# Query projections of an attention and expert kernel: from three split products over 128 rows to raw fp32 products over 64 rows

## The chip, the cores and the metric

The kernel runs on one core of one Trainium2 chip. A core has five engines that run side by side, each with its own instruction stream in a fixed order: TensorE (matrix products, PE in the profile, its loading of the stationary operand PEld), VectorE (DVE), ScalarE (ACT), GpSimd (POOL) and SyncE (SP, which issues loads). The metric is device time in microseconds (us) of one execution. Three runs of the kernel before took 596.02, 597.88 and 600.78 us; the median is 597.88.

## What is computed

```python
def phi(x):                                    # q, k, v: 4 batches x 8 heads x 576 x 64
    proj = np.einsum('bhsd,df->bhsf', x, w_phi)            # w_phi: 64 x 128
    proj = proj - np.max(np.abs(proj), axis=-1, keepdims=True)
    return np.concatenate([np.exp(proj), np.exp(-proj)], axis=-1)
q_p, k_p = phi(q), phi(k)
kv = np.einsum('bhsf,bhsd->bhfd', k_p, v)
z = np.sum(k_p, axis=2)
x = np.einsum('bhsf,bhfd->bhsd', q_p, kv) / (np.einsum('bhsf,bhf->bhs', q_p, z)[..., None] + 1e-06)
...                                            # heads joined: x is 4 x 576 x 512
gate = sigmoid(causal depthwise convolution of x, 5 taps)
x = (gate * (x @ w_val)) @ w_out
...                                            # one of 8 experts for each token, by running argmax
out = p[e] * (np.maximum(x @ w1[e], 0.0) @ w2[e])
```

The change is in `proj` of the queries alone. All inputs and results are fp32.

## The kernel before

The 4 x 576 tokens are 18 tiles of 128. `qT` and `kT` lie with the channels (8 heads x 64) on the rows, so a tile `raw` is 128 rows x 4 chunks x 128 tokens, and each chunk holds two heads one above the other. `wraw` holds `w_phi` twice on its diagonal (128 x 256, zeros elsewhere), so that one product over 128 rows projects both heads of a chunk. A half tile (`hh`) is four heads: two chunks, a result `pj` of 128 tokens x 512 in one bank of PSUM.

**Keys.** For each half tile two products of `raw` with `wraw` (line 129) in raw fp32, then on VectorE the largest absolute value (`m`, line 132) and its subtraction (`pp`, line 134), on ScalarE two exponentials (`ex`), and on TensorE `kv` (line 159), products of 64 columns, which add up over a batch.

**Queries.** The same projection, but each operand is split in two parts in a shorter format (fp32r): `split` casts a raw tile on ScalarE (`qkh`, line 49) and subtracts on GpSimd (`qkl`, line 52), and `wb_hi` and `wb_lo` are the parts of `wraw`. Three products then stand for one: hi x hi, hi x lo, lo x hi. A half tile takes six products of 128 rows, 128 stationary and 256 moving columns. After `m` and `pp` come four transposes (`tp`, line 186), the exponentials, the numerator and denominator (`num`, line 198, 64 columns) and the division. When both halves of a tile are done, `xp` (line 225) transposes its rows.

**Mixing.** Beside the queries run the convolution (VectorE, GpSimd, ScalarE), `vps` (line 400, x times `w_val` in three split products) and `yps` (line 535, gate times `w_out`). Small products `lpp`, `lps` and `wps` make the logits; `lpp` (line 432) writes one of four groups of 32 columns in each product. Then tokens are sorted by expert, gathered, and the expert stage (`hp`, line 857, and `op`, line 871) runs to the end.

**What sets the order.** `run` walks through the half tiles, first all keys, then all queries: the projection of half tile i + 3, the transposes of i + 1, the numerator of i, and some of the mixing. A scheduler then orders each engine's instructions by when it thinks that their operands are ready, so the order on an engine is not the order in the text. `pj` of the queries has two banks (`ps_p`, `bufs=2`), one for each half; `raw` has four buffers, and a tile's load is issued three tiles ahead (`loads_to`).

Of the kernel before, what the change touches and what calls it, by code (L numbers as in the profile page):

```python
# [8 lines left out]
F32 = mybir.dt.float32  # L9
F32R = mybir.dt.float32r  # L10
# [9 lines left out]
B, H, S, DH, DF = 4, 8, 576, 64, 128  # L20
T, D, E, FF, KC = 2304, 512, 8, 1024, 5
NT = T // 128
# [15 lines left out]
def body(ctx, tc, qT, kT, v1, wbd, w_val, conv_w, w_out, w_gl, w1, w2, out):  # L38
    nc = tc.nc
    V, A, G, PE, SP = nc.vector, nc.scalar, nc.gpsimd, nc.tensor, nc.sync  # L40
# [7 lines left out]
    def hi_of(eng, hi, src):  # L48
        (A.copy if eng is A else eng.tensor_copy)(hi, src)  # L49

    def lo_of(eng, lo, src, hi):
        eng.tensor_tensor(lo, src, hi.bitcast(F32), ALU.subtract)  # L52
# [21 lines left out]
    ap = attx.enter_context(tc.tile_pool(name="ap", bufs=1))  # L74
    ps_p = psx.enter_context(tc.tile_pool(name="ps_p", bufs=2, space=PSUM))
    ps_a = psx.enter_context(tc.tile_pool(name="ps_a", bufs=2, space=PSUM))
    ps_c = psx.enter_context(tc.tile_pool(name="ps_c", bufs=1, space=PSUM))
    ps_b = psx.enter_context(tc.tile_pool(name="ps_b", bufs=3, space=PSUM))

    wraw = ap.tile([128, 256], F32, name="wraw")  # L80
    wb_hi = ap.tile([128, 256], F32R, name="wb_hi")
    wb_lo = ap.tile([128, 256], F32R, name="wb_lo")

    raw_t, hl_t, v_t = {}, {}, {}

    def load(nm, t):
        if t >= NT or (nm, t) in raw_t:
# [14 lines left out]
        v_t[t] = mp.tile([128, H * VW], F32, tag=("gp", "gv")[t % 2], name="v", bufs=2)  # L102
        SP.dma_start(v_t[t], v1[t * 128:(t + 1) * 128, :])

    def split(nm, t):

        if t >= NT or (nm, t) in hl_t or nm == "k":
            return
        hi = ap.tile([128, 4, 128], F32R, tag="qkh", name="qkh", bufs=2)
        lo = ap.tile([128, 4, 128], F32R, tag="qkl", name="qkl", bufs=2)  # L110
        hi_of(A, hi, raw_t[nm, t])
        lo_of(G, lo, raw_t[nm, t], hi)
        hl_t[nm, t] = (hi, lo)

    def proj(nm, t, hh):
        raw = raw_t[nm, t]
        if nm == "k" and hh == 1:
            pj = ps_b.tile([128, 4, 128], F32, tag="b", name="pj")
        else:
            pj = ps_p.tile([128, 4, 128], F32, tag="pj", name="pj")  # L120
        for cc in range(2):
            c = 2 * hh + cc
            o = pj[:, 2 * cc:2 * cc + 2, :].rearrange("p h f -> p (h f)")
            prods = ((raw, wraw),)
            if (nm, t) in hl_t:
                hi, lo = hl_t[nm, t]
                prods = ((hi, wb_hi), (hi, wb_lo), (lo, wb_hi))
            for i, (st, mv) in enumerate(prods):
                PE.matmul(o, lhsT=st[:, c, :], rhs=mv, start=(cc == 0 and i == 0),  # L129
                          stop=(cc == 1 and i == len(prods) - 1), skip_group_check=True)  # L130
        m = ap.tile([128, 4], F32, tag="m", name="m", bufs=3)
        V.tensor_reduce(m, pj, axis=AX.X, op=ALU.max, apply_absolute_value=True)  # L132
        pp = ap.tile([128, 4, 128], F32, tag="pp", name="pp", bufs=3)
        V.tensor_tensor(pp, pj, m.unsqueeze(2).to_broadcast([128, 4, 128]), ALU.subtract)  # L134
        return pp
# [9 lines left out]
    def pk(t, hh):  # L145
        kp_t[t, hh] = both_exp(proj("k", t, hh))
# [32 lines left out]
    def pq(t, hh):  # L179
        pq_t[t, hh] = proj("q", t, hh)  # L180
# [63 lines left out]
    def bg(n, m=0):  # L244
        for i in range(n + m):
            if bgq and i < n:
                bgq.pop(0)()
            elif bg2 and len(done) == 4:
                bg2.pop(0)()
# [302 lines left out]
    st = {"step": 0, "credit": 0.0}  # L552
# [28 lines left out]
    order = []  # L581
# [4 lines left out]
    ahead = {i: (i + LF) // 2 for i in range(-LF, len(items))}  # L586

    def loads_to(i):
        for kind, t in order[:i + 1]:
            load(kind, t)  # L590
# [14 lines left out]
    def run(nbg, rate):  # L605
        n = len(items)
        txq = []
        for i in range(-LF, n + 3):
            st["step"] += 1
            if i == 1:  # L610
                setup_small()
            if 1 < i <= 5:
                setup_w("val", w_val, i - 2)
            if 0 <= i + LF < n:
                kind, t, hh = items[i + LF]
                if hh == 0:
                    loads_to(ahead[i] + 3)
                    for z in order[:ahead[i] + 2]:
                        split(*z)
                if kind == "k":  # L620
                    pk(t, hh)
                else:
                    pq(t, hh)
            if 0 <= i + 1 < n and items[i + 1][0] == "q":
                tq(*items[i + 1][1:])
            while txq and txq[0][0] <= i:
                t = txq.pop(0)[1]
                tx(t)
                if t % 2 == 1:
                    push_mix(t // 2)  # L630
            if 0 <= i < n:
                back(i)
                if items[i][0] == "q" and items[i][2] == 1:
                    txq.append((i + 2, items[i][1]))
            bg(*nbg(i))
            fill(rate(i))
# [3 lines left out]
    make_identity(nc, ident)  # L640
    load_v(0)
    loads_to(1)
    hi_of(V, wb_hi, wraw)
    lo_of(V, wb_lo, wraw, wb_hi)
    route_consts()
    run(lambda i: (0, 0) if i < 0 else ((i + 1) * 13 // 10 - i * 13 // 10, 0) if i < 36 else (5, 2), lambda i: 2.2 if i > 38 else 0)
    attx.close()
# [5 lines left out]
    for item in vq:  # L653
        what, z = item[3] or (None, 0)
# [84 lines left out]
    lo = t_([128, NT], "lo", BF16)  # L739
# [16 lines left out]
    for t in range(NT):  # L756
        pin(PE.matmul(tab.rearrange("p a c -> p (a c)"), lhsT=ohl[:, t, :], rhs=ohc[:, t].rearrange("p a c -> p (a c)"),
                  start=(t == 0), stop=(t == NT - 1)))
# [214 lines left out]
```

## Time and profile before

| what | value |
|---|---|
| profiled execution | 596.02 us, of which 594.2 us of span |
| key stage, 0 to 88.0 us | TensorE busy 81.35 us |
| query stage, 88.0 to 238.2 us (first to last query product) | TensorE busy 148.47 us |
| rest of the mixing, to 313.2 us | TensorE busy 74.41 of 75.00 us |
| gathers, to 331 us | TensorE busy 14.11 of 17.80 us |
| experts, to the end | TensorE busy 251.60 of 263.00 us |

A record of the timeline says when an instruction started and how long it took from its start to its end. TensorE's steps overlap, so the distance from one start to the next, and not the duration, is what a step costs the stream. A shape such as 128*64 128x65 is 128 rows x 64 stationary columns, and 128 rows x 65 moving columns. Equal records that follow each other are merged (x32); the start is that of the first.

### The profile page before, as it was taken

Reading aid. Unit: us, or ns where it says so; the run is one execution under the profiler, and the core shown is the slowest. Engines: PE = TensorE matmul, PEld = TensorE weight load, DVE = VectorE, ACT = ScalarE, POOL = GpSimd, SP = SyncE. Lnnn points to the kernel's source line nnn. Section 1 sums busy time; section 2 is a strip of 40 time slices with the busy share of each in tenths; the row PEclk is TensorE's granted clock in tenths of the full one; section 3 lists DMA queues with packets and bytes.
Section 4 is the critical chain, followed back from the end, with each engine's and each line's share of the span. In section 5 each row is a group of like instructions: output and inputs, shape, how many; then the busy total and the mean of one; then the engine's idle time right before and its main releaser. Section 6 shows DMA issues by size and latency. Waiting matters only on the chain. (4 is left out here: it accounts for less than half of the span.)

```text
span 594.2 us, 13524 instructions
## 1 busy us (share of the span) xinstructions
PE 569.9 (96%) x5477; PEld 495.5 (83%) x5478; DVE 365.2 (61%) x726; ACT 313.1 (53%) x573; POOL 238.0 (40%) x258
## 2 busy tenths in 40 slices
PE   7999999999999999999997999999999999999993
PEld 6777788898889889888784988889889899898982
DVE  5888689478687876569613766555666656452110
ACT  3767566466665575565323656445655646541210
POOL 2453055388778885583124022322340322311001
PEclk9999999899999999999998899999999999999997
DMA  8934431111101000221524887758668649620000
GB/s 281 311 99 122 130 107 49 32 33 38 36 4 35 3 38 21 72 77 48 198 90 132 302 268 217 239 190 269 210 211 272 202 138 291 203 95 36 17 19 36
DMA packets 46017, 76.82 MB, mean 129 GB/s; under 512 B 3839, under 2 KB 22399, under 8 KB 45952
## 3 DMA queue, kind: packets, MB, share of 16 engines
q1 hardware_dynamic: 39840, 60.55, 32.8%
q0 software_dynamic: 3520, 10.58, 4.7%
q10 hardware_dynamic: 2592, 4.79, 2.1%
q8 instruction: 45, 0.74, 0.5%
q14 instruction: 20, 0.16, 0.1%
HBM read 66.39 MB, written 10.56 MB: 130 GB/s over the span
## 5 line engine op out<-in xcount | busy, mean ns | idle before, releaser
L857 PE MATMUL hp<-xh,w1h 128*128 128x256 f32 (+1 forms) x320 | 94.6, 296 | 1.4 <-DVE hlo L860 0.8
L857 PE MATMUL hp<-xh,w1l 128*128 128x256 f32 (+1 forms) x320 | 93.8, 293 | 0.0
L857 PE MATMUL hp<-xl,w1h 128*128 128x256 f32 (+1 forms) x320 | 93.3, 294 | 0.0
L815 POOL DMA_INDIRECT xg<-y_d,gidx x22 | 36.7, 1669 | 98.5 <-DVE p L838 83.4
L877 POOL DMA_INDIRECT out<-osb,sidx x22 | 28.0, 1271 | 115.1 <-ACT osb L876 69.0
L871 PE MATMUL op<-w2h,hh 128*128 128x512 f32 x176 | 69.5, 400 | 1.0 <-ACT hh L859 0.9
L52 DVE TENSOR_TENSOR w2l<-wraw,w2h 128x1024 fp32r<-128x1024 f32 x40 | 48.8, 1223 | 34.5 <-ACT w2h L49 34.3
L860 DVE SCALAR_TENSOR_TENSOR hlo<-hp,hh 128x256 fp32r<-128x256 f32 (+1 forms) x80 | 34.2, 446 | 55.4 <-ACT hh L859 55.4
L871 PE MATMUL op<-w2l,hh 128*128 128x512 f32 x176 | 68.2, 393 | 0.0
L871 PE MATMUL op<-w2h,hlo 128*128 128x512 f32 x176 | 67.0, 394 | 0.0
L857 PEld LDWEIGHTS hp<-xh,w1h 128*128 128x128 f32 x320 | 61.2, 191 | 3.9 <-DVE hlo L860 1.2
L52 DVE TENSOR_TENSOR w1l<-wraw,w1h 128x1024 fp32r<-128x1024 f32 x40 | 48.7, 1251 | 24.1 <-ACT w1h L49 24.1
L857 PEld LDWEIGHTS hp<-xh,w1l 128*128 128x128 f32 x320 | 61.1, 191 | 1.4
L857 PEld LDWEIGHTS hp<-xl,w1h 128*128 128x128 f32 x320 | 60.7, 191 | 0.0
L132 DVE TENSOR_REDUCE m<-pj 128x4 f32<-128x512 f32 x72 | 49.3, 686 | 18.4 <-PE pj L129 17.5
L266 DVE SCALAR_TENSOR_TENSOR acc<-xT,tfs,acc 128x256 f32<-128x256 f32 (+1 forms) x112 | 53.8, 485 | 10.8 <-ACT acc L264 9.7
L859 ACT ACTIVATE hh<-hp 128x256 fp32r<-128x256 f32 (+1 forms) x80 | 31.4, 403 | 53.8 <-PE hp L857 53.6
L49 ACT CAST w2h<-wraw 128x1024 fp32r<-128x1024 f32 x40 | 41.8, 1050 | 31.7 <-DMA wraw<-w 22.3
L49 ACT CAST w1h<-wraw 128x1024 fp32r<-128x1024 f32 x40 | 40.3, 1049 | 24.6 <-DMA wraw<-w 24.5
L159 PEld LDWEIGHTS kv<-v,ex 128*64 128x64 f32 (+1 forms) x1280 | 40.7, 137 | 14.7 <-issue 6.8
L134 DVE TENSOR_TENSOR pp<-pj,m 128x512 f32<-128x512 f32 x72 | 49.4, 686 | 4.4 <-PE tp L186 1.8
L159 PE MATMUL kv<-v,ex 128*64 128x65 f32 (+1 forms) x1280 | 46.1, 224 | 3.0 <-DVE kvsb L171 1.4
(194 smaller groups left out, 1332.5 us busy)
## 6 DMA issues: line engine op xcount, KB each, us to landing
wraw<-w SPq DMA_DIRECT2D x80, 512.0 KB, 4.5
v<-v SPq DMA_DIRECT2D x18, 260.0 KB, 3.2
y_d<-ysb ACTq DMA_DIRECT2D x18, 260.0 KB, 2.1
raw<-qT SPq DMA_DIRECT2D x18, 256.0 KB, 2.9
raw<-kT SPq DMA_DIRECT2D x17, 256.0 KB, 4.2
wr<-w_val SPq DMA_DIRECT2D x4, 512.0 KB, 5.9
wr<-w_out SPq DMA_DIRECT2D x4, 512.0 KB, 6.9
xg<-y_d,gidx POOLq DMA_INDIRECT x22, 5.4
```

Source lines behind the costliest of these rows:

```text
L49: (A.copy if eng is A else eng.tensor_copy)(hi, src)
L52: eng.tensor_tensor(lo, src, hi.bitcast(F32), ALU.subtract)
L132: V.tensor_reduce(m, pj, axis=AX.X, op=ALU.max, apply_absolute_value=True)
L134: V.tensor_tensor(pp, pj, m.unsqueeze(2).to_broadcast([128, 4, 128]), ALU.subtract)
L159: PE.matmul(kv_ps[b][blk // 7][mh * 64:mh * 64 + 64, (blk % 7) * VW:(blk % 7 + 1) * VW], lhsT=kp_t[t, hh][off:off + n, sg, h, mh * 64:mh * ...
L266: W["tap"] = V.scalar_tensor_tensor(acc[c], xs, cw[:, kk, c:c + 1], acc[c], ALU.mult, ALU.add)
L815: G.indirect_dma_start(out=xg, out_offset=None, in_=y_d, in_offset=bass.IndirectOffsetOnAxis(ap=gc, axis=0))
L857: PE.matmul(hp[:, 0:n], lhsT=wt[:, k, f * 128:(f + 1) * 128], rhs=xt[:, k, 0:n], start=(i == 0), stop=(i == 11))
L859: A.activation(hh[:, f, 0:n], hp[:, 0:n], AF.Relu)
L860: low = V.scalar_tensor_tensor(hlo[:, f, 0:n], hp[:, 0:n], 0.0, hh[:, f, 0:n].bitcast(F32), ALU.max, ALU.subtract)
L871: PE.matmul(op, lhsT=ht[:, f, sl], rhs=wt[:, f, :], start=(i == 0), stop=(i == 23))
L877: G.indirect_dma_start(out=out, out_offset=bass.IndirectOffsetOnAxis(ap=scols[j], axis=0), in_=osb, in_offset=None, bounds_check=T - 1, oo ...
```

## The change

The splits of the queries are gone: `split`, `qkh`, `qkl`, `wb_hi` and `wb_lo`, one cast on ScalarE and one subtraction on GpSimd for each tile, and two operations on VectorE at the start. The queries are projected in raw fp32. The host lays `qT` out so that chunk c holds head c in rows 0 to 63 and head 4 + c in rows 64 to 127. Each product takes 64 rows of the array, 128 stationary columns (the tokens) and 128 moving columns (`w_phi`), and the two halves of a tile write two banks. All eight products of a tile are issued with its first half, in turn upper and lower. The keys are as they were.

```diff
@@ -78,10 +78,8 @@
     ps_b = psx.enter_context(tc.tile_pool(name="ps_b", bufs=3, space=PSUM))
 
     wraw = ap.tile([128, 256], F32, name="wraw")
-    wb_hi = ap.tile([128, 256], F32R, name="wb_hi")
-    wb_lo = ap.tile([128, 256], F32R, name="wb_lo")
-
-    raw_t, hl_t, v_t = {}, {}, {}
+
+    raw_t, v_t = {}, {}
 
     def load(nm, t):
         if t >= NT or (nm, t) in raw_t:
@@ -102,32 +100,29 @@
         v_t[t] = mp.tile([128, H * VW], F32, tag=("gp", "gv")[t % 2], name="v", bufs=2)
         SP.dma_start(v_t[t], v1[t * 128:(t + 1) * 128, :])
 
-    def split(nm, t):
-
-        if t >= NT or (nm, t) in hl_t or nm == "k":
-            return
-        hi = ap.tile([128, 4, 128], F32R, tag="qkh", name="qkh", bufs=2)
-        lo = ap.tile([128, 4, 128], F32R, tag="qkl", name="qkl", bufs=2)
-        hi_of(A, hi, raw_t[nm, t])
-        lo_of(G, lo, raw_t[nm, t], hi)
-        hl_t[nm, t] = (hi, lo)
+    pj_t = {}
+
+    def products(nm, t, hh):
+        raw = raw_t[nm, t]
+        if nm == "k":
+            pool, tag = ((ps_p, "pj"), (ps_b, "b"))[hh]
+            pj = pj_t[hh] = pool.tile([128, 4, 128], F32, tag=tag, name="pj")
+            for cc in range(2):
+                o = pj[:, 2 * cc:2 * cc + 2, :].rearrange("p h f -> p (h f)")
+                PE.matmul(o, lhsT=raw[:, 2 * hh + cc, :], rhs=wraw, start=(cc == 0), stop=(cc == 1), skip_group_check=True)
+        elif hh == 0:
+
+            for z in range(2):
+                pj_t[z] = ps_p.tile([128, 4, 128], F32, tag="pj", name="pj")
+            for c in range(4):
+                for z in range(2):
+                    rows = slice(z * 64, z * 64 + 64)
+                    PE.matmul(pj_t[z][:, c, :], lhsT=raw[rows, c, :], rhs=wraw[rows, z * DF:z * DF + DF],
+                              start=(c == 0), stop=(c == 3), skip_group_check=True)
 
     def proj(nm, t, hh):
-        raw = raw_t[nm, t]
-        if nm == "k" and hh == 1:
-            pj = ps_b.tile([128, 4, 128], F32, tag="b", name="pj")
-        else:
-            pj = ps_p.tile([128, 4, 128], F32, tag="pj", name="pj")
-        for cc in range(2):
-            c = 2 * hh + cc
-            o = pj[:, 2 * cc:2 * cc + 2, :].rearrange("p h f -> p (h f)")
-            prods = ((raw, wraw),)
-            if (nm, t) in hl_t:
-                hi, lo = hl_t[nm, t]
-                prods = ((hi, wb_hi), (hi, wb_lo), (lo, wb_hi))
-            for i, (st, mv) in enumerate(prods):
-                PE.matmul(o, lhsT=st[:, c, :], rhs=mv, start=(cc == 0 and i == 0),
-                          stop=(cc == 1 and i == len(prods) - 1), skip_group_check=True)
+        products(nm, t, hh)
+        pj = pj_t.pop(hh)
         m = ap.tile([128, 4], F32, tag="m", name="m", bufs=3)
         V.tensor_reduce(m, pj, axis=AX.X, op=ALU.max, apply_absolute_value=True)
         pp = ap.tile([128, 4, 128], F32, tag="pp", name="pp", bufs=3)
@@ -615,8 +610,6 @@
                 kind, t, hh = items[i + LF]
                 if hh == 0:
                     loads_to(ahead[i] + 3)
-                    for z in order[:ahead[i] + 2]:
-                        split(*z)
                 if kind == "k":
                     pk(t, hh)
                 else:
@@ -640,8 +633,6 @@
     make_identity(nc, ident)
     load_v(0)
     loads_to(1)
-    hi_of(V, wb_hi, wraw)
-    lo_of(V, wb_lo, wraw, wb_hi)
     route_consts()
     run(lambda i: (0, 0) if i < 0 else ((i + 1) * 13 // 10 - i * 13 // 10, 0) if i < 36 else (5, 2), lambda i: 2.2 if i > 38 else 0)
     attx.close()
@@ -946,7 +937,9 @@
     import concourse.bacc as bacc
     from concourse.bass_utils import run_bass_kernel_spmd
 
-    def chan(a):
+    def chan(a, paired=False):
+        if paired:
+            a = a[:, [h // 2 + h % 2 * (H // 2) for h in range(H)]]
         return np.ascontiguousarray(a.transpose(1, 3, 0, 2).reshape(H * DH, T))
 
     ones = np.ones((B, S, H, 1), dtype=v.dtype)
@@ -955,7 +948,7 @@
     wbd[:DH, :DF] = w_phi
     wbd[DH:, DF:] = w_phi
     arrays = {
-        "qT": chan(q), "kT": chan(k), "v1": v1, "wbd": wbd,
+        "qT": chan(q, True), "kT": chan(k), "v1": v1, "wbd": wbd,
         "w_val": np.ascontiguousarray(moe_w_val).view(np.int64),
         "conv_w": np.ascontiguousarray(moe_conv_w.reshape(KC, 4, 128).transpose(2, 0, 1).reshape(128, KC * 4)).view(np.int64),
         "w_out": np.ascontiguousarray(moe_w_out).view(np.int64),
```

The scheduler moves instructions. Two places on TensorE show how. The first is the first query tile, at the border of keys and queries. In the names, `kv` are the key sums, `pj` the projections with their buffer's number; before:

```order
L159 MATMUL kv1_1162<-v_984,ex_1223 64x65 x2
L129 MATMUL pj_1351<-wb_hi_94,qkh_1276 128x256
L129 MATMUL pj_1351<-wb_lo_95,qkh_1276 128x256
L129 MATMUL pj_1351<-wb_hi_94,qkl_1277 128x256
L129 MATMUL pj_1351<-wb_hi_94,qkh_1276 128x256
L129 MATMUL pj_1351<-wb_lo_95,qkh_1276 128x256
L129 MATMUL pj_1351<-wb_hi_94,qkl_1277 128x256
L159 MATMUL kv1_1162<-v_984,ex_1254 64x65 x12
```

and now, where `pj_1339` is the upper half's result (heads 0 to 3) and `pj_1340` the lower half's:

```order
L154 MATMUL kv1_1158<-v_980,ex_1219 64x65 x2
L120 MATMUL pj_1339<-wraw_93,raw_1111 128x128
L120 MATMUL pj_1340<-wraw_93,raw_1111 128x128
L120 MATMUL pj_1339<-wraw_93,raw_1111 128x128
L120 MATMUL pj_1340<-wraw_93,raw_1111 128x128
L120 MATMUL pj_1339<-wraw_93,raw_1111 128x128
L120 MATMUL pj_1340<-wraw_93,raw_1111 128x128
L120 MATMUL pj_1339<-wraw_93,raw_1111 128x128
L120 MATMUL pj_1340<-wraw_93,raw_1111 128x128
L154 MATMUL kv1_1158<-v_980,ex_1250 64x65 x12
```

The products of both halves now stand at the place of the first half's, in turn, as in the text.

The second place is the sixth query tile on TensorE; `num` is the numerator of an earlier half tile, `tp` and `xp` are transposes. Before:

```order
L129 MATMUL pj_1874<-wb_hi_94,qkh_1741 128x256
L129 MATMUL pj_1874<-wb_lo_95,qkh_1741 128x256
L129 MATMUL pj_1874<-wb_hi_94,qkl_1742 128x256
L198 MATMUL num_1718<-kvsb_526,ex_1662 64x65 x16
L186 MATMUL tp_1756<-ident_61,pp_1655 128x128 x4
L225 MATMUL xp_1764<-ident_61,x_1618 128x128 x2
L129 MATMUL pj_1973<-wb_hi_94,qkh_1741 128x256
L129 MATMUL pj_1973<-wb_lo_95,qkh_1741 128x256
L129 MATMUL pj_1973<-wb_hi_94,qkl_1742 128x256
```

and now (`pj_1822` is the upper half's, `pj_1823` the lower half's):

```order
L181 MATMUL tp_1715<-ident_61,pp_1622 128x128 x4
L220 MATMUL xp_1723<-ident_61,x_1586 128x128 x2
L120 MATMUL pj_1822<-wraw_93,raw_1505 128x128 x4
L193 MATMUL num_1747<-kvsb_522,ex_1674 64x65 x16
L181 MATMUL tp_1782<-ident_61,pp_1667 128x128 x4
L120 MATMUL pj_1823<-wraw_93,raw_1505 128x128 x4
L220 MATMUL xp_1848<-ident_61,x_1677 128x128 x2
```

Here the scheduler has parted the two halves: four products of the upper half, other work, then four of the lower. Over the 18 tiles, five have all eight products in turn as in the first place (one of them with `num` before the last two), one has four in turn and four in pairs of one half, three have four of one half directly before four of the other, one has three directly before four, and in eight other work stands between the halves' blocks. From the first to the last query product the array's shape (whole, 64 columns, 32 columns, 64 rows) changes 97 times in the order before and 119 times in this; if 64 rows and the whole array are counted as one shape, 89 times.

## Rows read from the trace of the kernel before

**Rows 1.** The page, part 1: busy us, share of the span, instructions.

```profile
PE 569.9 (96%) x5477; PEld 495.5 (83%) x5478; DVE 365.2 (61%) x726; ACT 313.1 (53%) x573; POOL 238.0 (40%) x258
```

**Rows 2.** Stretches: start:end, length, busy (count) by engine, TensorE clock, DMA share, GB/s.

```profile
0.00:88.00 88.00, 81.35 (x1337) 65.16 (x1337) 66.95 (x111) 57.44 (x103) 31.62 (x52) 1.00 0.57 175
88.00:238.20 150.20, 148.47 (x1913) 132.83 (x1911) 114.18 (x274) 91.27 (x199) 109.88 (x122) 0.99 0.10 30
238.20:313.20 75.00, 74.41 (x611) 60.39 (x610) 44.25 (x126) 34.15 (x70) 31.81 (x42) 1.00 0.29 100
...
108.80:112.20 3.40, 3.40 (x26) 3.25 (x26) 1.46 (x4) 0.97 (x3) 0.00 (x0) 0.50 0.19 53
112.20:116.00 3.80, 3.80 (x57) 3.41 (x57) 2.67 (x7) 2.86 (x6) 1.33 (x2) 1.00 0.00 0
```

**Rows 3.** Groups by line, 88 to 238.2 us: count, busy us, mean ns, idle before.

```profile
L129 PE MATMUL pj<-wb_hi,qkh 128*128 128x256 f32 x72 | 22.7, 315 | 1.7 <-DVE pp L134 1.7
L129 PE MATMUL pj<-wb_lo,qkh 128*128 128x256 f32 x72 | 20.6, 287 | 0.0
L129 PE MATMUL pj<-wb_hi,qkl 128*128 128x256 f32 x72 | 20.4, 284 | 0.0
```

**Rows 4.** Waits of TensorE, 88 to 238.2 us: total us, times, longest.

```profile
PE pj L129 <- DVE pp L134: 1.7, 4, 0.6
```

**Rows 5.** Timeline of TensorE, two places: start us, us.

```profile
87.99 0.39 PE L129 MATMUL pj<-wb_hi,qkh 128*128 128x256 f32 x1
...
88.89 1.15 PE L159 MATMUL kv<-v,ex 128*64 128x65 f32 x32
89.97 0.39 PE L129 MATMUL pj<-wb_hi,qkh 128*128 128x256 f32 x1
...
237.17 0.28 PE L129 MATMUL pj<-wb_hi,qkh 128*128 128x256 f32 x1
...
237.88 0.39 PE L535 MATMUL yps<-wout_h,gh 128*128 128x512 f32 x1
```

**Rows 6.** Timeline of TensorE around the steps of nine columns.

```profile
104.08 1.85 PE L372 MATMUL wps<-wgl,woT 128*128 128x9 f32 x16
105.78 0.36 PE L129 MATMUL pj<-wb_hi,qkh 128*128 128x256 f32 x1
```

**Rows 7.** Timeline of TensorE: raw products, runs over 64 rows, column quarters.

```profile
26.78 1.13 PE L129 MATMUL pj<-wraw,raw 128*128 128x256 f32 x4
27.84 1.15 PE L159 MATMUL kv<-v,ex 64*64 64x65 f32 x32
28.92 1.13 PE L129 MATMUL pj<-wraw,raw 128*128 128x256 f32 x4
...
34.59 2.35 PE L159 MATMUL kv<-v,ex 64*64 64x65 f32 x68 [0.76 <-DVE kvsb L171]
36.87 0.48 PE L129 MATMUL pj<-wraw,raw 128*128 128x256 f32 x1
...
75.92 3.17 PE L159 MATMUL kv<-v,ex 64*64 64x65 f32 x96
79.02 0.48 PE L129 MATMUL pj<-wraw,raw 128*128 128x256 f32 x1
...
149.14 0.64 PE L432 MATMUL lpp<-gv,wl 128*32 128x256 f32 x8
149.71 0.39 PE L129 MATMUL pj<-wb_hi,qkh 128*128 128x256 f32 x1
```

**Rows 8.** Groups by line, whole span: the keys' projection.

```profile
L129 PE MATMUL pj<-wraw,raw 128*128 128x256 f32 x144 | 42.2, 425 | 3.6 <-DMA raw<-kT 3.6
```

**Rows 9.** Groups by line, 88 to 238.2 us: the queries' splits.

```profile
L49 ACT CAST qkh<-raw 128x512 fp32r<-128x512 f32 x16 | 10.1, 632 | 2.6 <-POOL tmw L323 1.2 <-PE pj L129 1.0 <-issue 0.4
L52 POOL TENSOR_TENSOR qkl<-raw,qkh 128x512 fp32r<-128x512 f32 x16 | 21.0, 1310 | 4.9 <-ACT qkh L49 4.9
```

## The prediction

> **What bounds the kernel now.** First the busy shares: TensorE 96%, VectorE 61% [rows 1]. Then the stages. The query stage, from the first query product at 88.0 us to the last at 238.2 us, has 148.47 us of TensorE work in 150.20 us, the rest of the mixing after it 74.41 in 75.00 [rows 2]. A busy TensorE need not be one at its peak, so I next read its waits there: one line, four waits for VectorE's `pp`, 1.7 us in all [rows 4]. No wait there names ScalarE, GpSimd or a load. So TensorE bounds the query stage by its own instruction stream, and what is put into that stream or taken out arrives at the end of the stage one for one. The next stage is filled by the same engine, and the gathers and the expert stage come after it, so the end moves as well. This case is a count of TensorE steps.
>
> The steps must be read as start to start, since their durations overlap: six query products between steps that also use the whole array take 237.88 - 237.17 = 0.71 us, 0.118 each, though each is recorded as about 0.28 [rows 3, 5].
>
> **The change part by part.**
>
> *Taken out of TensorE.* 3 x 72 = 216 records of query products [rows 3] at 0.118 = **-25.5 us**.
>
> *Put in.* 18 tiles x 8 = 144 raw products, each over 64 rows and 128 columns. A raw fp32 product runs as two records: the keys' 72 left 144 [rows 8]. So 288 records. The price of one: four raw records of 256 columns between column-split steps take 27.84 - 26.78 = 1.06 us [rows 7]; six query products in such a place take 88.89 - 87.99 = 0.90, against 0.71 elsewhere [rows 5], so 0.19 of it is entry and exit, and a record is (1.06 - 0.19) / 4 = 0.22 for 256 columns, 0.11 for 128. Loading 128 stationary columns sets the same floor: 16 steps of nine moving columns took 105.78 - 104.08 = 1.70 us, 0.106 each [rows 6]. Half the rows buys nothing by itself: 32 `kv` records over 64 rows take 28.92 - 27.84 = 1.08 us, and 32 over 128 rows 89.97 - 88.89 = 1.08 [rows 5, 7]. So 288 x 0.11 = **+31.7 us** if none overlap.
>
> *Shape switches.* Each time the array's shape changes (whole, column-split, 64 rows) something is lost. The `kv` runs of 68 and 96 records took 2.28 and 3.10 us, so a record is 0.82 / 28 = 0.029; 32 records alone took 1.08, so 68 should take 1.08 + 36 x 0.029 = 2.13. The 0.15 over is the one change from 64 to 128 rows inside that run [rows 7]. The order of the programs, counted from the first to the last query product, has 97 changes of shape before and 119 after: 22 x 0.15 = **+3.3 us**. The other bound: if a 64-row step beside a whole-array step costs nothing, there are 89, and it is -8 x 0.15 = -1.2. I take +3.3, since the row just used is a change of rows and has its price. The Trainium skill (TensorEngine Tiling (Array Packing), Key Properties) says that a change of tiling mode drains TensorE while a change of tile within a mode doesn't; that speaks against this change, and its first half agrees with the 0.15.
>
> *Overlap of the two halves.* No row shows two row halves at work together. The nearest shows column parts: eight `lpp` records of 256 columns, for four quarters of the columns, took 149.71 - 149.14 = 0.57 us, 0.07 each, where a whole-array record of 256 columns takes 0.22 [rows 7]. So parts of the array do run together. Bounds: nothing, or half of everything. It can only happen where the two halves' products stand next to each other, and the order decides that: they alternate for five and a half of the 18 tiles; the other tiles have four of one half in a row, then four of the other, mostly with `num`, `tp` or `vps` in between. I take full overlap where they alternate: 5.5 tiles x 16 records x 0.11 / 2 = **-4.8 us**.
>
> *Waits.* A query product still waits until VectorE has read the bank of the tile before; there are two banks as before, and behind the waiting product stand the transposes and `num`, since TensorE keeps its order. Now 1.7 us [rows 4]. It may go, or double: VectorE's own work is unchanged, but its order is new. I take 0, with -1.7 and +1.7 as bounds.
>
> *ScalarE, GpSimd, loads.* In the query stage 10.1 us of casts and 21.0 us of subtractions go [rows 9]. Worth 0: no TensorE wait there names either engine [rows 4]. The two `wb` operations at the start go too; the first product then waits 3.6 us for a load [rows 8], which covers them. A raw query tile is now held until TensorE's products instead of GpSimd's subtraction; with four buffers and loads three tiles ahead, that costs 0.
>
> *Sum.* -25.5 + 31.7 + 3.3 - 4.8 = **+4.7 us**. The profiled execution took 596.02 us (594.2 us of span and 1.8 around it), the fastest of three; the median, 597.88, lies 1.9 above. So 600.7 on that execution, **602.6 us** as a median.
>
> **The rivals.**
>
> *No overlap at all* (slower): 64-row steps of the two halves run one after the other even where they alternate, since the weight loads, or two banks written at once, hold them apart. For it: no row has two row halves together. Against it: `lpp` and `num` overlap by columns. It decides as soon as less than a quarter of the overlap comes, since 1% (about 6 us, what a measurement can tell from no change) is 603.9. Price 4.8: 607.4 us.
>
> *Overlap also for blocks of four* (less slow): three tiles have four of one half directly before four of the other, a fourth has three and four; if TensorE looks far enough ahead to start the second block beside the first, about 3.5 x 0.88 = 3.1 us more are saved: 599.5 us. For it: the eight `lpp` records belong to four products of two records each, and 0.57 us is far less than 5 steps of 0.22, which a strict first in, first out of both records of each product would need [rows 7]. The Trainium skill (TensorE: Matmul & The Clock Gate, Part 3) says that matmuls start and end in program order and only weight loads are pulled ahead, so by it this rival gives nothing; the `lpp` rows don't fit that simply.
>
> *The clock.* For 3.40 us, from 108.8, the granted clock was 0.5, that is 1.2 GHz: 26 matmuls, then 57 in the next 3.80 us at 2.4 GHz [rows 2]. Just before it TensorE was in the steps of nine columns that begin at 104.08 [rows 6]. If half-used array steps bring two more such stretches, +3.4: 606.0 us. Against it: the clock stood at 1.00 from 0 to 88 us, with `kv` over 64 rows in it [rows 2, 7].
>
> *All 18 tiles overlap* (faster): a factor of two on every query product. 18 x 0.88 = 15.8 instead of 4.8: 591.6 us. The Trainium skill (TensorEngine Tiling, Theoretical Speedup) gives up to 2x for a contraction of 64 rows, which is this case; no run here shows it. Against it: in eight tiles `num`, `tp` or `vps` stand between the halves, mostly in another shape. That the change does less than it says, pairs in a third of the tiles only, is already in the forecast.
>
> **How the numbers follow.** Forecast (overlap where they alternate) 0.46, no overlap 0.18, blocks of four 0.22, clock 0.09, all tiles 0.05. Predicted time: that of the likeliest, 602.6 us. Its own uncertainty is the waits (1.7), the spread of the three runs (2) and the cheaper switches (4.5 lower), so 598 to 605. The range for 8 in 10 takes in no overlap with its waits (607.4 + 1.7) and blocks of four with some cheaper switches: **597.5 to 609**. Slower by over 1% means above 603.9: no overlap nearly whole (0.17), the clock (0.07), a quarter of the forecast (0.12): 0.36. Faster by over 1% means below 591.9: 0.04, from the last rival. Within 1%: 0.60.
>
> **What would show it.** In the profile after: the query products as 288 records of 128 columns over 64 rows; in alternating tiles the 16 records in about 0.9 us, with starts in pairs; in a block of four, eight records in about 0.9 us and 0.2 for entry and exit; the query stage 155 us long instead of 150.2, and the stages after it as long as before. It would be wrong if alternating products didn't pair, if the stage had new waits for `pp` of more than 2 us, or if `hp` began at another distance from the last query product.

## The result, and the profile after

The changed kernel took **604.32 us** in the median of 20 runs, the kernel before 597.47 in 20. The ratio is **1.0111**, with a 95% interval of 1.0085 to 1.0137. The forecast was 602.6 us with a range of 597.5 to 609. Some executions ran in a slower state; medians here and below are of all runs, and ratios leave those out, so a ratio isn't exactly the quotient of two medians. The profiled execution took 604.19 us with a span of 602.5, against 596.02 and 594.2 before.

The page's first part after, which answers to [rows 1]:

```profile
PE 576.6 (96%) x5549; PEld 500.1 (83%) x5550; DVE 360.9 (60%) x724; ACT 303.4 (50%) x555; POOL 214.5 (36%) x240
```

TensorE has 72 records more (288 raw ones instead of 216) and 6.7 us more to do. ScalarE and GpSimd lost 18 instructions each. GpSimd lost 23.5 us of work, ScalarE 9.7.

The stretches after, as in [rows 2]: query stage, the rest of the mixing, the longest stretch at the lower clock level, and a shorter one in the key stage.

```profile
88.20:244.40 156.20, 153.46 (x2009) 135.45 (x2006) 112.64 (x275) 83.64 (x186) 91.34 (x108) 0.97 0.11 32
244.40:319.90 75.50, 75.06 (x587) 61.10 (x586) 43.66 (x124) 33.74 (x68) 29.98 (x40) 1.00 0.28 100
...
106.90:117.10 10.20, 10.20 (x67) 9.38 (x67) 2.84 (x6) 2.60 (x7) 0.00 (x0) 0.50 0.10 27
...
35.20:38.60 3.40, 3.40 (x54) 3.07 (x51) 3.40 (x6) 2.42 (x5) 1.28 (x1) 0.50 0.35 76
```

The query stage grew from 150.20 to 156.20 us and TensorE still fills it. But its mean granted clock is 0.97 instead of 0.99: the one stretch at 0.50 (1.2 GHz) was 3.40 us long before and is 10.20 us now. Another one, of 3.40 us, lies in the key stage at 35.20, where the clock stood at 1.00 before. No query product has run by then, and most kernels below have one of 3.4 or 6.8 us there, the kernel before with a widened gate product among them, so the change of the products isn't shown to be its cause. The stage after is 0.5 longer. The gathers were 0.4 shorter, and from the first `hp` to the end it took 270.1 us instead of 268.3.

The query products as one group, against the 216 records of [rows 3], and TensorE's waits in the stage, against [rows 4]:

```profile
L120 PE MATMUL pj<-wraw,raw 64*128 64x128 f32 x288 | 34.6, 291 | 1.9 <-issue 1.3 <-DVE pp L129 0.6
```

```profile
PE pj L120 <- issue: 1.3, 1, 1.3
PE num L193 <- ACT ex L135: 0.9, 2, 0.5
PE pj L120 <- DVE pp L129: 0.6, 1, 0.6
```

The waits went from 1.7 to 2.8 us. The timeline of TensorE shows all four kinds of place that the prediction told apart:

```profile
88.24 1.16 PE L120 MATMUL pj<-wraw,raw 64*128 64x128 f32 x16
89.33 3.01 PE L154 MATMUL kv<-v,ex 128*64 128x65 f32 x94
93.66 1.13 PE L120 MATMUL pj<-wraw,raw 64*128 64x128 f32 x8 [1.31 <-issue]
...
101.51 1.16 PE L120 MATMUL pj<-wraw,raw 64*128 64x128 f32 x8
102.59 1.15 PE L193 MATMUL num<-kvsb,ex 128*64 128x65 f32 x30
...
104.51 1.95 PE L367 MATMUL wps<-wgl,woT 128*128 128x9 f32 x16
106.32 0.63 PE L181 MATMUL tp<-ident,pp 128*128 128x128 f32 x4
106.88 2.07 PE L120 MATMUL pj<-wraw,raw 64*128 64x128 f32 x8
108.89 0.69 PE L193 MATMUL num<-kvsb,ex 128*64 128x65 f32 x6
109.51 3.58 PE L367 MATMUL wps<-wgl,woT 128*128 128x9 f32 x16
...
160.53 1.71 PE L120 MATMUL pj<-wraw,raw 64*128 64x128 f32 x16
162.16 1.15 PE L193 MATMUL num<-kvsb,ex 128*64 128x65 f32 x32
```

- **Alternating halves**: at 88.24, 16 records in 1.09 us from start to next start. At 211.6 the single starts are 211.589, 211.596, then 211.803, 211.809, then 211.914, 211.921: pairs 6 or 7 ns apart.
- **A block of four of one half**: at 101.51, eight records take 102.591 - 101.506 = 1.085 us, as long as 16 alternating ones. The single starts give 0.214 us for the first step, 0.112 for each of the others and 0.201 for the last one, up to `num`: 0.10 of entry and 0.09 of exit.
- **Two blocks of four that touch**: at 160.53, 16 records in 1.63 us, not in twice 1.085. The trace doesn't name a record's block, but the starts fall into two rows with the steps of a lone block. Read so, the second block's first record starts at 161.080, 6 ns behind the fifth of the first, and its next two (161.293, 161.405) stand 4 ns ahead of the first block's last two (161.297, 161.409).
- **The lower clock**: the block at 106.88 took 2.01 us, 16 gate products of nine columns at 109.51 took 3.51, against 1.81 at 104.51.

### The profile page after: what moved, and what is told of

Same layout as the page of the kernel before. It is cut to its first block, busy times and chain, and to the rows that moved or that the text cites. A ratio compares the mean times of both kernels' runs of the same rounds, so it can differ in the third digit from the quotient of the medians.

```text
span 602.5 us, 13613 instructions
## 1 busy us (share of the span) xinstructions
PE 576.6 (96%) x5549; PEld 500.1 (83%) x5550; DVE 360.9 (60%) x724; ACT 303.4 (50%) x555; POOL 214.5 (36%) x240
## 5 line engine op out<-in xcount | busy, mean ns | idle before, releaser
L49 ACT CAST w1h<-wraw 128x1024 fp32r<-128x1024 f32 x40 | 40.3, 1048 | 29.8 <-DMA wraw<-w 29.8
```

## The experiments

Beside the ratio I use two numbers of every kernel, means over the runs that its ratio rests on: the time at the lower clock, 2 x (1 - mean granted clock) x span, and the time less half of that, called *at full clock*. This is a way to split a time, not a second measurement: where TensorE waits, the clock costs less. Each experiment's ratio is taken to runs of the kernel before beside it, in three series whose medians were 595.89, 597.40 and 595.55 us. The row of the kernel before gives its median from the runs of the result, and means over the three series.

| kernel | median us | ratio to before (95%) | lower clock | at full clock |
|---|---|---|---|---|
| before | 597.47 | | 19.3 | 586.9 |
| the change | 604.32 | 1.0111 (1.0085 to 1.0137) | 26.7 | 590.1 |
| paired order | 591.65 | 0.9920 (0.9891 to 0.9950) | 18.1 | 582.6 |
| raw products on whole rows | 604.28 | 1.0134 (1.0098 to 1.0170) | 16.3 | 596.1 |
| change, gate product widened | 597.21 | 1.0007 (0.9981 to 1.0032) | 15.3 | 589.7 |
| before, gate product widened | 597.14 | 1.0035 (1.0007 to 1.0063) | 15.7 | 590.0 |
| half by half | 610.46 | 1.0233 (1.0163 to 1.0303) | 25.0 | 597.8 |
| half by half, gate widened | 606.50 | 1.0162 (1.0092 to 1.0231) | 16.9 | 598.0 |
| paired, gate widened | 592.66 | 0.9920 (0.9885 to 0.9956) | 13.5 | 585.9 |
| ScalarE's part of the splits kept | 605.53 | 1.0163 (1.0078 to 1.0249) | 33.3 | 589.6 |
| GpSimd's part kept | 622.68 | 1.0439 (1.0368 to 1.0509) | 55.3 | 595.1 |
| both parts kept | 622.19 | 1.0325 (1.0214 to 1.0435) | 37.0 | 598.0 |
| both kept, gate widened | 613.69 | 1.0260 (1.0172 to 1.0349) | 29.7 | 597.2 |

The last column has a second uncertainty. In the expert stage, where nothing was edited, TensorE's waits for `hh` differ from profile to profile, from none to 4.8 us (0.9 before, 1.1 in the change). So I also compare one stage alone, from the first query product to the end of the mixing, with half of its time at the lower clock taken off: 225.35 - 1.7 = 223.7 us before, 232.02 - 5.1 = 226.9 in the change, each from one profile.

### Is the order of the halves what counts?

Paired order: the products keep the order they are written in, so that 119 of 126 neighbours alternate instead of 42.

```diff
-                for z in range(2):
+                for z in (1, 0):
...
-                    PE.matmul(...)
+                    with tc.high_priority(offset=400 if (c, z) != (0, 1) else 0):
+                        mm = PE.matmul(...)
+                    if (c, z) != (0, 1):
+                        tc.keep_in_program_order(mm)
```

> The changed kernel, with the eight query products of a tile kept in turn (lower, upper, lower, ...) by ordering edges and a higher scheduling priority, so that 119 of 126 neighbours inside a tile alternate instead of 42. Theory (time is the count of TensorE's steps, neighbouring halves overlap): a block of four takes 1.09 us and eight in turn 1.09 us as well, so the query products fall from 32.6 to about 21 us, and changes of shape from 119 to 104 (2 us more, partly the same thing): about 592 to 595 us, faster than both. Rival (the overlap seen in the changed kernel is given back as waits for VectorE, since both banks must now be free before a tile starts): 600 to 604 us, with new waits of the query products for pp of 5 us or more. Rival (the changed kernel is slow because of its half-clock stretches): they stay, and no more than 3 us is gained.

Its group of query products, and two stretches, query stage and rest of the mixing:

```profile
L121 PE MATMUL pj<-wraw,raw 64*128 64x128 f32 x288 | 24.3, 287 | 1.8 <-issue 1.3 <-PE xp L223 0.5
```

```profile
89.80:229.80 140.00, 135.23 (x1940) 120.19 (x1936) 107.12 (x264) 79.63 (x178) 84.63 (x100) 1.00 0.12 36
229.80:308.30 78.50, 77.91 (x656) 63.47 (x654) 48.26 (x136) 36.55 (x76) 36.70 (x48) 1.00 0.27 96
```

The same 288 records keep TensorE busy for 24.3 us instead of 34.6, and both stretches together take 218.50 us instead of 231.70. The clock stayed at 1.00. At a ratio of 0.9920, with an interval clear of 1, this order beats both kernels. 7.5 us of the 12 that it gains on the change come at full clock, the rest from less time at the lower one. TensorE waited 4.8 us in the query stage instead of 2.8, so little of the overlap was given back.

Half by half is the opposite: each half's four products are issued where the kernel before had that half, so 4 neighbours alternate, and the shape changes 133 times instead of 119.

```diff
-        elif hh == 0:
-            for z in range(2):
-                pj_t[z] = ps_p.tile([128, 4, 128], F32, tag="pj", name="pj")
+        else:
+            z = hh
+            pj_t[z] = ps_p.tile([128, 4, 128], F32, tag="pj", name="pj")
...
```

> Same products as the change, 288 records on 64 rows, but each half's four products of a step are issued together, the other half's at another place, so that almost no records of the two halves stand next to each other (4 alternations instead of 42, 133 changes of shape instead of 119). Theory 'the overlap of neighbours of two halves pays for the extra records': every four products cost about 1.085 us as the lone blocks of the change do, 36 x 1.085 = 39 us of query products from start to start instead of 32.6, first query product to tab about 238 us instead of 231.9, the run about 609 to 612 us (604 to 607 if it should have no half-clock stretch of 10 us near 107). Rival 'the halves' overlap is worth little in the run': query products as they were within 2 us, 603 to 606 us.

```profile
L118 PE MATMUL pj<-wraw,raw 64*128 64x128 f32 x288 | 40.3, 286 | 0.6 <-DVE pp L127 0.6
```

It took 610.46 us, where the count had 609 to 612, and TensorE is busy with these products for 40.3 us instead of 34.6. But the count had 604 to 607 for the case without a long stretch at the lower clock, and the profile has only one of 3.4 us in the query stage; part of the rest is a wait of the expert stage:

```profile
PE op L860 <- ACT hh L848: 3.5, 2, 2.3
```

At full clock it is 7.7 us above the change, and 2.4 of that are this wait (3.5 against 1.1). From the first query product to the end of the mixing it took 234.5 - 1.7 = 232.8 us, 5.9 more than the change. 14 more changes of shape at the prediction's 0.15 are 2.1, which leaves about 3.8 us for the overlap. Counted from each query product's start to the next start of TensorE, without waits and with steps at the lower clock halved, the products take 37.8 us here, 31.5 in the change and 22.6 in the paired order; by that the overlap in the change is worth up to 6.3. So it is worth some 4 to 6 us, and the runs don't give it more closely.

Whole rows: the kernel before without splits, its raw products over 128 rows, 144 records of 256 columns.

```diff
...
     def split(nm, t):
-        if t >= NT or (nm, t) in hl_t or nm == "k":
-            return
+        return
...
-            if (nm, t) in hl_t:
-                hi, lo = hl_t[nm, t]
-                prods = ((hi, wb_hi), (hi, wb_lo), (lo, wb_hi))
...
```

> Splits taken out of the queries as in the change, but raw fp32 products over all 128 rows with the doubled w_phi, as the keys have them: one half of the change alone, without 64-row steps. Theory (count of steps): 72 products x 2 records x 0.216 = 31.1 us in place of 25.5, changes of shape 96 against 97: about 5.6 us slower than before, 603 us. Rival (taking the casts off ScalarE and the subtractions off GpSimd is worth something by itself): less than 3 us slower than before, or faster. Rival (row halves are the cost of the change): as fast as before.

As a median it equals the change, since it spends 10 us less at the lower clock. At full clock it stands 6.0 us above the change, but most of that isn't the halves' doing: waits for `hh` in the expert stage took 3.7 us, against 1.1. From the first query product to the end of the mixing it took 228.9 us, all at 1.00: 2.0 more than the change, which is what the halves save with the overlap that they have, and 5.2 more than before, where the count gave 5.6. A relief by the casts and subtractions taken out doesn't show.

### The clock

The gate product (`wps`) streams nine columns. Here its weights are padded with zeros to 128, in the change, in before, and in two others.

```diff
-        wgl = mp.tile([128, 4, E + 1], F32, name="wgl")
-        SP.dma_start(wgl, w_gl)
+        wgl = mp.tile([128, 4, 128], F32, name="wgl")
+        G.memset(wgl, 0.0)
+        SP.dma_start(wgl[:, :, 0:E + 1], w_gl)
...
-                        wps = ps_b.tile([128, E + 1], F32, tag="b", name="wps")
+                        wps = ps_b.tile([128, 128], F32, tag="b", name="wps")
...
```

> The changed kernel, with the 9 moving columns of the wps products padded to 128 with zeros: as many steps, bound by the same loads of 128 stationary columns (0.112 us each), so the same TensorE time at full clock. The order differs a little (114 changes of shape, 51 alternating neighbours). Theory (the half-clock stretch of 10.2 us at 106.9 us comes of the steps of nine columns, which keep the array nearly idle): the stretch is gone or 3.4 us, 3 to 5 us faster than the changed kernel: 599 to 600 us. Rival (it comes of the 64-row products): the stretch stays, 602 to 604 us.

The change with the gate product widened, the timeline of TensorE at the place of the 10.20 us, and the same stretch of time:

```profile
103.20 2.05 PE L368 MATMUL wps<-wgl,woT 128*128 128x128 f32 x16
105.09 0.60 PE L181 MATMUL tp<-ident,pp 128*128 128x128 f32 x4
105.62 1.16 PE L120 MATMUL pj<-wraw,raw 64*128 64x128 f32 x8
106.70 0.45 PE L193 MATMUL num<-kvsb,ex 128*64 128x65 f32 x8
107.08 2.05 PE L368 MATMUL wps<-wgl,woT 128*128 128x128 f32 x16
```

```profile
106.90:117.10 10.20, 9.63 (x148) 8.66 (x146) 5.31 (x12) 3.50 (x8) 1.27 (x1) 1.00 0.19 54
```

Sixteen steps of 128 columns take 105.09 - 103.20 = 1.89 us, hardly more than the 1.81 of nine columns, and the clock stays at 1.00: 148 matmuls in those 10.20 us instead of 67. The gain is 7 us in the median, more than the 3 to 5 expected, and by the split nearly all of it is clock (15.3 us at the lower level instead of 26.7, at full clock 0.4 apart). From the first query product to the end of the mixing it took 226.1 us instead of 232.0, of which the lower clock explains 5.1. The order came out a little different (114 changes of shape, 51 alternations), so the rest may be that.

> The kernel before with the same padding of wps; its order is as before. Theory: its half-clock stretch of 3.4 us at 108.8 us goes, 1.7 us faster than before, 595.8 us. Rival (the stretch has another cause): it stays, and the time is that of before.

In the kernel before, the 3.40 us at 0.50 went as well, and the mixing was 0.45 us shorter. But no gain came of it: the expert stage had a new wait.

```profile
PE op L872 <- ACT hh L860: 4.1, 2, 3.9
```

It stood at 0.9 us before, and these 3.2 us are as much as the difference at full clock (590.0 against 586.9), though the order is that of before. The wait is 3.3 us in the paired order and 4.4 in the widened change. I didn't find out what sets it.

> The kernel of the half-by-half blocks, with the gate product (9 moving columns) widened by zeros to 128 columns. Theory 'the half-clock stretch near 107 us belongs to the gate product with its 9 columns': no stretch near 107, about 39 us of query products, first query product to tab about 236 us, 605 to 608 us. Rival 'it belongs to the 64-row products': a half-clock stretch beside the gate products stays or others come among the blocks, and the time is that of the unwidened blocks within 2 us.

Half by half with the gate widened: no stretch at 0.50 in the query stage, and 606.50 us, as the theory had it. So 64-row blocks, of which this kernel has 36, don't bring the stretch by themselves, and in three kernels (the change, before, half by half) it was gone when the nine columns were widened. But nine columns don't always bring it either. The whole rows have 16 of these steps at 104.77 and at 108.51, the paired order has them too, and both keep a clock of 1.00 through the query stage:

```profile
101.89 1.63 PE L370 MATMUL wps<-wgl,woT 128*128 128x9 f32 x14
...
105.61 2.18 PE L370 MATMUL wps<-wgl,woT 128*128 128x9 f32 x18
```

How long it lasts differs as well: half by half, with nine columns, has one of 3.4 us at 109.6, the change one of 10.2. What decides that isn't shown; the 64-row products may have a part in it.

> All query products in alternating pairs (117 of 126), and the gate product widened to 128 columns by zeros. Theory 'order and clock are separate gains, and the paired order without widening has already no half-clock stretch near 107': 590 to 593 us, within 2 us of the paired order alone (591.7), ratio to before 0.990 to 0.994. Rival 'the two gains add': 585 to 588 us, the 6 us that the widening took off the change once more.

The two gains don't add: 592.66 us, at the ratio of the paired order alone. The time at the lower clock fell by 4.6 us, but the order changed once more: `pj` then waits 6.0 us in place of 1.8, most of it for `pp`:

```profile
L121 PE MATMUL pj<-wraw,raw 64*128 64x128 f32 x288 | 25.6, 288 | 6.0 <-DVE pp L132 4.5 <-issue 1.3
```

### Were the splits worth nothing?

Both parts of the queries' splits are computed as before and read by nothing.

```diff
...
+    def split(nm, t):
+        if t >= NT or (nm, t) in hl_t or nm == "k":
+            return
+        hi = ap.tile([128, 4, 128], F32R, tag="qkh", name="qkh", bufs=2)
+        lo = ap.tile([128, 4, 128], F32R, tag="qkl", name="qkl", bufs=2)
+        hi_of(A, hi, raw_t[nm, t])
+        lo_of(G, lo, raw_t[nm, t], hi)
+        hl_t[nm, t] = (hi, lo)
...
+                    for z in order[:ahead[i] + 2]:
+                        split(*z)
```

> The change, with the query splits of before still computed on ScalarE and GpSimd (10.1 us and 21.0 us of work) and not used by anything. 126 changes of shape instead of 119 and 33 alternations instead of 42. Theory 'the splits were hidden and taking them out is worth nothing': the count gives +0.7 us for 7 more changes and about +1 us for the alternations lost, so 604 to 607 us, first query product to tab 232 to 235 us. Rival 'taking the splits out relieved a wait by several us': 609 us or more, with new waits of the query products or of the attention stage's products on ScalarE or GpSimd.

My theory (worth nothing) fell. The runs spread from 613 to 626 us, the ratio rests on two of the four (613.17 and 619.82), and that kernel's profile, of the slowest run, had a TensorE wait of 3.9 us near 92. The next two keep one part each: ScalarE's (`hi_of` alone), or GpSimd's (`lo_of(G, lo, raw, raw)` alone).

> The change with only ScalarE's half of the query splits kept and used by nothing (18 casts of 0.60 us), none on GpSimd; 119 changes of shape and 42 alternations as in the change. Theory 'the loss with both splits kept comes from GpSimd, whose subtractions stretch VectorE's int32 operations of the table work beside them (0.42 us beside an idle GpSimd, 1.51 us beside a busy one) and so delay the maxima and differences of the keys': 603 to 606 us, the operation of 0.42 us as short as there, TensorE's wait near 92 us about 1.5 us, no half-clock stretch of over 11 us. Rival 'ScalarE is the engine that was relieved': 610 us or more, and a wait of about 4 us near 92.

> The change with only GpSimd's half of the query splits kept and used by nothing (18 subtractions of 1.28 us, here of the raw tile from itself), none on ScalarE; 125 changes of shape, 37 alternations. Theory 'GpSimd beside VectorE': the table's int32 operations near 90 us take about 1.5 us instead of 0.42 wherever a subtraction lies beside them, TensorE's wait near 92 us 3 to 4 us instead of 1.5, 608 to 622 us. Rival 'ScalarE': 604 to 607 us (6 more changes of shape), the wait near 92 as in the change.

The timeline with ScalarE's part kept: VectorE, GpSimd, TensorE.

```profile
89.74 0.42 DVE L317 TENSOR_SCALAR tfw<-wr 128x512 int32<-128x512 int32 x1
90.08 1.28 DVE L135 TENSOR_REDUCE m<-pj 128x4 f32<-128x512 f32 x2
91.28 0.68 DVE L321 SCALAR_TENSOR_TENSOR tbw<-wr,tfw 128x512 int32<-128x512 int32 x1
91.87 1.28 DVE L137 TENSOR_TENSOR pp<-pj,m 128x512 f32<-128x512 f32 x2
...
91.31 1.78 POOL L52 TENSOR_TENSOR wout_l<-tfw,wout_h 128x512 fp32r<-128x512 f32 x1 [2.21 <-ACT wout_h L49]
...
92.66 1.13 PE L128 MATMUL pj<-wraw,raw 64*128 64x128 f32 x8 [0.89 <-issue]
```

The same with GpSimd's part kept:

```profile
90.20 1.26 DVE L317 TENSOR_SCALAR tfw<-wr 128x512 int32<-128x512 int32 x1
91.39 1.27 DVE L135 TENSOR_REDUCE m<-pj 128x4 f32<-128x512 f32 x2
92.59 1.55 DVE L321 SCALAR_TENSOR_TENSOR tbw<-wr,tfw 128x512 int32<-128x512 int32 x1
94.06 1.27 DVE L137 TENSOR_TENSOR pp<-pj,m 128x512 f32<-128x512 f32 x2
...
89.69 1.49 POOL L52 TENSOR_TENSOR qkl<-raw 128x512 fp32r<-128x512 f32 x1
91.14 1.44 POOL L52 TENSOR_TENSOR wout_l<-tfw,wout_h 128x512 fp32r<-128x512 f32 x1
92.55 1.03 POOL L52 TENSOR_TENSOR qkl<-raw 128x512 fp32r<-128x512 f32 x1
...
94.83 1.13 PE L128 MATMUL pj<-wraw,raw 64*128 64x128 f32 x8 [3.00 <-issue]
```

Two int32 operations of the table work take 1.26 and 1.55 us beside a busy GpSimd, 0.42 and 0.68 without the query subtractions. The two `pp` behind them on VectorE come 2.2 us later, and the next query product starts as soon as the first `pp` is done (0.69 us each, so at 92.56 and 94.75, 0.1 us ahead of the product). So TensorE waits 3.0 us instead of 0.9 (in the change, whose `tbw` took 1.10 us beside GpSimd's `wout_l`, 1.3). What follows is larger than the wait; stretches of the kernel with GpSimd's part, from the product on:

```profile
94.83:96.10 1.27, 1.27 (x10) 1.13 (x10) 1.14 (x3) 0.42 (x1) 0.00 (x0) 1.00 0.00 0
96.10:103.00 6.90, 6.90 (x30) 5.95 (x28) 3.09 (x5) 2.92 (x6) 1.30 (x2) 0.50 0.14 40
103.00:117.00 14.00, 14.00 (x106) 12.11 (x105) 7.14 (x14) 2.79 (x5) 4.56 (x4) 0.50 0.08 23
117.00:137.10 20.10, 20.10 (x156) 18.14 (x157) 4.39 (x11) 4.34 (x11) 2.30 (x2) 0.50 0.09 25
```

1.3 us after the wait the granted clock falls to 0.50 and stays there for 41.0 us, with TensorE busy throughout. By the split, 14.3 of the 19 us by which this kernel is slower than the change are clock (55.3 - 26.7, halved), 5.0 are not; its order has 6 more changes of shape and 5 fewer alternations than the change, at the prediction's prices an estimated 1.5 of these. ScalarE's part costs nothing that can be told at full clock: 589.6 us, against 590.1. Its mean is 2.8 us above the change's, and that is clock: the stretch at 106.6 lasted 13.7 us, where the theory allowed 11.

The Trainium skill (SBUF — State Buffer, Who interferes with whom) says that VectorE and GpSimd share a pair of ports, that an operation of VectorE in a two-port mode, or with two SBUF inputs while GpSimd reads SBUF, locks it against GpSimd, and that the later one is blocked outright, while a reduction isn't. The trace agrees: `tfw`, begun at 90.20, ends at 91.46, some 0.3 us after GpSimd's subtraction of 89.69 to 91.18, and each of the two `m` takes the same time in both kernels.

> Both splits kept and unused, and the gate product widened by zeros from 9 to 128 columns; 123 changes of shape, 45 alternations. Theory 'the long half-clock stretch of the kernel with both splits follows the 4 us wait, and is held up by the gate products': the 4 us wait stays, half-clock stretches before 160 us of at most 10 us together, 604 to 608 us. Rival 'the wait alone makes the long stretch': a half-clock stretch of 30 to 45 us behind the wait as without the widening, 615 to 625 us.

Both parts kept with a wide gate product: a wait of 3.9 us again, and a stretch at 0.50 of 17.1 us behind it, instead of 41.0. Neither theory had that: with the wide gate product the stretch is shorter, and behind the wait there is still a long one. A wait is followed by a fall elsewhere too: in the kernel before with the widened gate, a wait of 3.91 us for `hh` ends at 358.71, and from 359.4 the clock is at 1.2 GHz for 3.4 us. That the wait is the cause is argued from this order in time alone. What raises the clock again is open.

## Why the prediction was right, and where it wasn't

- **Records taken out and put in, changes of shape (+9.5 without overlap)**: right in sign, a little large. Half by half, nearly without overlap, stands 10.9 us above before at full clock, but 2.6 of that are the expert stage's waits for `hh` (3.5 against 0.9). From the first query product to the end of the mixing it took 9.2 us more than before, or 7.1 without the 2.1 for its 14 extra changes of shape.
- **A record 0.11 us, a change of shape 0.15**: 0.112 measured, and 0.19 for the entry and exit of a block together. These are two changes of shape, so one costs nearer 0.10 there, and the 22 of the sum nearer 2 us than 3.3.
- **Overlap where the halves alternate (-4.8)**: the mechanism is shown, by starts 6 or 7 ns apart and by 16 records in the time of eight. The term left out a part, since the **rival of touching blocks** was partly right. It put 0.88 us on such a tile, and 2.17 - 1.63 = 0.54 came, about 1.9 us over the 3.5 tiles (4.8 + 1.9 = 6.7 by this count; the half-by-half run, with 4 to 6, doesn't bear out as much). With it the prediction's sum is +4.7 - 1.9 = +2.8, and at full clock the change stands 590.1 - 586.9 = **+3.2 us** above before, as it does from the first query product to the end of the mixing (226.9 - 223.7).
- **The clock (0 in the sum, a rival at 0.09)**: this step failed. The sum put nothing on the clock. The rival put two more stretches of 3.4 us on the change, +3.4 us; 7.3 us more at the lower clock came as a mean over the runs, **+3.7 us**, so its size was right. Its cause, half-used array steps, doesn't bring such a stretch alone. The stretch in the query stage was gone when the steps of nine columns were widened, which the prediction had seen in the rows just ahead of the earlier one; why it is three times as long in the change isn't shown, and part of the 7.3 lies elsewhere. In the profile 3.4 us of it are in the key stage, whose clock of 1.00 before the prediction had set against the rival.
- **The sum**: +3.2 and +3.7 are +6.9 us, where +4.7 was forecast. The sign and the range were right, partly by luck: the touching blocks that were left out and the clock that was put at nothing pull opposite ways. The ratio of 1.0111 lies on the 1% that divides "no change" from "slower", and its interval takes in both.
- **ScalarE, GpSimd and loads at 0**: right for ScalarE. For GpSimd the reason was wrong. No wait of the kernel before names it: there the two banks were filled one at a time, with `kv` and query products in turn [rows 5]. Even so its `tbw` of the same place, at 91.14, took 1.71 us beside GpSimd's `wout_l`. The change fills both banks at once and then runs 94 `kv` records, so the next product waits for `pp`, and a late VectorE shows. With GpSimd's subtractions left in, the change took 18 us more, most of it at the lower clock; taking them out paid for what the rest of the change had made possible. A hidden engine is hidden only in the order in which it was seen.
- **Waits (0, within 1.7 either way)**: +1.1 in the profile, inside the bounds.
- **No overlap (607.4) and all tiles (591.6)**: neither is what the change does, but both were tried: 610.46 with 14 more changes of shape and 591.65. In the latter some 4 us are from the clock, so the agreement is closer than the count deserves.

The row of the kernel before, for GpSimd's point:

```profile
91.14 1.71 DVE L318 SCALAR_TENSOR_TENSOR tbw<-wr,tfw 128x512 int32<-128x512 int32 x1
```

The Trainium skill (TensorE: Matmul & The Clock Gate, Part 3) says that matmuls keep the program's order in start and end. Here the second of two touching blocks starts its first record while the first has three records to go (161.080, beside 161.185, 161.297 and 161.409), if the records are told apart by their even steps. That doesn't fit the order in start. Which instruction of the program each record belongs to, the trace doesn't say.

## What to carry to other kernels

Half-row products pay only where the two halves stand next to each other in TensorE's own order: count the neighbours in that order before counting on a factor, and if a scheduler decides it, hold the pairs together. Before a hidden engine is costed at nothing, look at which instructions of a second engine grow beside it, and ask whether the change takes away the slack behind them. Read the granted clock of a stretch as a term of its own: here steps of nine columns took as long as steps of 128 columns, and widening them with zeros took the half-clock stretch of the query stage away in three kernels. That paid 7 us in the change, 4 half by half, and nothing in the kernel before, where the expert stage waited longer.

## What the runs showed of the hardware that was not expected

- 16 gate steps took 1.81 us with nine columns and 1.89 with 128, but in four kernels (before, the change, half by half, ScalarE's part kept) a stretch of 3.4 to 13.7 us at 1.2 GHz began 1.6 to 3.1 us after the first of a group of nine-column steps, and none in the query stage behind the wide ones alone. Two kernels (paired, whole rows) had the nine-column steps and no such stretch.
- After a TensorE wait of 3.0 us the clock was at 1.2 GHz for 41.0 us with the engine busy throughout; after waits of 0.9 and 1.3 us at the same place it stayed at 2.4 GHz for the next 13 us.
- Two blocks of four 64-row products, one for each half, overlap in their middle: 16 records in 1.63 us, where two separate blocks take 2.17.
